# A smaller share of a convolution's lane for VectorE, closed by a product that GpSimd's additions wait for

## The chip, the cores and the metric

The kernel runs on one core of one Trainium2 chip. The metric is device time in microseconds of one execution. The engines are named as the profile names them: PE (TensorE matmul, with PEld for its weight loads), DVE (VectorE), ACT (ScalarE), POOL (GpSimd) and SP (SyncE, which here only issues transfers).

## The reference

Two operations follow each other. A depthwise causal convolution over the sequence, with 7 taps for each of 8 heads (the taps are a softmax of the given weights, 24 channels to a head):

```python
w = softmax(weight)                                  # (8 heads, 7 taps)
x_pad = concat([zeros((B, 6, D)), x], axis=1)        # B=8, S=4096, D=192
out[b, s, h, g] = sum_k w[h, k] * x_pad[b, s + k, h, g]
```

Then a gated feed-forward layer on its 32768 rows of 192, with 1536 hidden columns:

```python
gate = maximum(x @ w_gate, 0)
val = x @ w_val
return (gate * val) @ w_out                          # float32, (32768, 192)
```

## The kernel before, in words

The sequence is cut into 16 units of 1024 positions (UNIT) of two batches at once: batch b lies on partitions 0 to 63, batch b + 4 on 64 to 127. The 192 channels are three planes of 64, so the convolved input of a unit is a tile xc of 128 x 3 x 1024 in f16, or 3072 columns when it is read flat (FLAT).

**A unit's work on PE** has two stages. `gate_val` makes, for each of two windows of 512 and each of 12 blocks f of hidden columns, the gate and the value products (line 468, six matmuls each) into two PSUM tiles. ACT takes the gate through Relu to gr (line 477), DVE multiplies gr with the value's PSUM tile into hT (line 478). Then `project_columns` runs three times (p = 0, 1, 2), 96 matmuls each (line 488), into one PSUM tile each. DVE turns each of these (line 502, `turn_out`) into the output tile, and SP stores it when the third is done. All PSUM tiles named ps come from one pool with four buffers that are taken in turn, so a tile waits until the fourth tile before it has been read.

**The convolution of units 2 to 15** is made two units ahead, beside the projections, in what the code calls a lane. POOL loads x (`lane_load`), copies it into another order (`lane_turn`, line 387), and SP issues eight DMA transposes that make x_r, with channels on partitions and positions along the free axis, plus a halo of 16. From x_r each tap is a shifted read times a scale that differs by partition. The 3072 columns are divided at LDVE:

- Columns 0 to LDVE are DVE's. ACT makes the first tap into acc in f32 (`lane_first`, line 434), DVE adds the six others with one instruction each and piece (`lane_rest`, line 445: in0 * scalar + in1, inputs x_r and acc). The last tap writes xc in f16. A piece ends at a plane's end, so LDVE = 1408 gives two pieces per tap, 1024 and 384 columns: 12 instructions, handed out one at a time by a generator.
- Columns LDVE to FLAT are ACT's and POOL's. ACT multiplies each tap into a tile of its own, prod0 to prod6 in f32 (`product`, line 414, pieces of 640 and 1024), and POOL adds prod1 to prod6 onto prod0 one after the other (`add`, line 423), the last sum going to xc.

**The order** is written out by hand (`manual_schedule`): every engine works off its instructions in the order in which the code emits them. In the loop over units a lane stands around the projections of unit u for unit u + 2: `lane_first` on ACT, and then after each `project_columns` the products of the taps in TAPS[p], STEPS[p] of the lane's instructions on DVE, and the transpose. So DVE has 3 steps, a transpose, 4 steps, a transpose, 5 steps, a transpose, and then the 24 multiplications of line 478 of the next unit. ACT emits tap 0 last. POOL's first addition of a lane (prod0 + prod1) is emitted at the start of the next unit, ahead of the halo copy, the two copies to x_p, the two loads of x_e, four more additions and the one into xc. Each prod tile has one buffer.

Units 0 and 1 get their convolution on PE from band matrices (`conv_dense`, `conv`), and the last unit has another projection (`project`, line 524). Lanes run in the units 0 to 13; unit 0's addition is emitted in unit 1, and so on. Unit 0's projections have convolution work of unit 1 between them, on PE and on ACT.

Of the kernel before, what the change touches and what calls it, by code (L numbers as in the profile page):

```python
# [10 lines left out]
ACTF = mybir.ActivationFunctionType  # L11
ALU = mybir.AluOpType
# [3 lines left out]
def kernel(  # L16
# [12 lines left out]
    nc = tc.nc  # L29
# [10 lines left out]
    WIN = 512  # L40
    NWIN = S // WIN
    SUB = 112
    STEPS = [3, 4, 5]
    TAPS = [(6, 5, 4), (3, 2), (1, 0)]
    GSUB = 5

# [2 lines left out]
    NUNIT = NB * S // UNIT  # L49
    HALO = 16  # L50
    FLAT = NCH * UNIT
    LDVE = 1408
    TILES = UNIT // 128
    GROUPS = [(0, [WIN * w + SUB * j for j in range(GSUB)]) for w in range(2)]
    second = [min(t, 2 * UNIT - SUB) for t in range(UNIT, 2 * UNIT, SUB)]
# [55 lines left out]
    for half, eng in ((0, nc.sync), (1, nc.scalar)):  # L111
        eng.dma_start(
            out=wr[64 * half : 64 * half + 64],
            in_=bass.AP(
                tensor=weight.tensor,
                offset=weight.offset + 2 * half * HQ * KW,
                ap=[[HQ * KW, 2], [0, 32], [1, HQ * KW]],
            ),
# [8 lines left out]
    for n in range(16):  # L127
        nc.tensor.matmul(  # L128
            out=ps[:, n % 2, :], lhsT=zeros[:, 0:128], rhs=zeros[:], start=True, stop=True
# [9 lines left out]
    for q in range(4):  # L139
        nc.gpsimd.affine_select(  # L140
            out=eye[32 * q : 32 * q + 32],
            in_=ones[32 * q : 32 * q + 32],
# [55 lines left out]
    tap = const.tile([128, NCH, KW], FP)  # L198

    def load_taps():  # L200
# [23 lines left out]
        out=prod[:],  # L224
        in0=bass.AP(tensor=e0.tensor, offset=e0.offset, ap=[e0.ap[0], [0, HQ], [1, BW], [1, KW]]),
# [115 lines left out]
    xes, xrs, accs, prods = {}, {}, {}, {}  # L341
# [53 lines left out]
    def pieces(lo, hi):  # L395


        while lo < hi:
            c, t = lo // UNIT, lo % UNIT
            n = min(UNIT - t, hi - lo)  # L400
            yield lo, n, c, t
            lo += n

    def shifted(u, c, k, t, n):
        o = HALO - KW + 1 + k + t
        return xrs[u][:, c, o : o + n]

    def flat(u):
        return xc[u][:].rearrange("p c t -> p (c t)")

    def product(u, k):
        prods[u, k] = apool.tile([128, FLAT - LDVE], FP, name=f"prod{k}")
        for at, n, c, t in pieces(LDVE, FLAT):
            nc.scalar.activation(  # L414
                out=prods[u, k][:, at - LDVE : at - LDVE + n],
                in_=shifted(u, c, k, t, n),
                func=ACTF.Copy,
                scale=tap[:, c, k : k + 1],
            )

    def add(u, k):
        p0 = prods[u, 0]
        nc.gpsimd.tensor_tensor(  # L423
            out=p0[:] if k < KW - 1 else flat(u)[:, LDVE:FLAT],
            in0=p0[:],
# [4 lines left out]
    def lane_first(u):  # L430
        accs[u] = apool.tile([128, LDVE], FP, name="acc")
        xc[u] = xcpool.tile([128, NCH, UNIT], F16, name="xc")
        for at, n, c, t in pieces(0, LDVE):
            nc.scalar.activation(  # L434
                out=accs[u][:, at : at + n],
                in_=shifted(u, c, 0, t, n),
                func=ACTF.Copy,
                scale=tap[:, c, 0:1],
            )

    def lane_rest(u):
        acc = accs.pop(u)
        for k in range(1, KW):
            for at, n, c, t in pieces(0, LDVE):
                nc.vector.scalar_tensor_tensor(  # L445
                    out=(flat(u) if k == KW - 1 else acc)[:, at : at + n],
                    in0=shifted(u, c, k, t, n),
                    scalar=tap[:, c, k : k + 1],
                    in1=acc[:, at : at + n],
                    op0=ALU.mult,  # L450
                    op1=ALU.add,
                )
                yield

    def gate_val(u, w):
        h = hpool.tile([128, NFF, 2, WIN], F16, name="hT")
        xcb = xc[u]
        for f in range(NFF):
            if u == 0 and w == 0 and f == 7:
                conv_dense(1)  # L460
            pss = [psum.tile([128, 2, 512], FP, name="ps") for _ in range(2)]
            order = [(i, c) for i in range(2) for c in range(NCH)]
            if u == 0 and w == 0 and f == 0:
                order.sort(key=lambda ic: ic[1])
            for i, c in order:
                W = (Wg, Wv)[i]
                for st in range(2):
                    nc.tensor.matmul(  # L468
                        out=pss[i][:, st, :],
                        lhsT=W[64 * st : 64 * st + 64, c, 128 * f : 128 * (f + 1)],  # L470
                        rhs=xcb[64 * st : 64 * st + 64, c, WIN * w : WIN * (w + 1)],
                        start=(c == 0),
                        stop=(c == NCH - 1),
                        tile_position=(64 * st, 0),
                    )
            gr = gpool.tile([128, 2, WIN], F16, name="gr")
            nc.scalar.activation(out=gr[:], in_=pss[0][:], func=ACTF.Relu)  # L477
            nc.vector.tensor_tensor(out=h[:, f], in0=gr[:], in1=pss[1][:], op=ALU.mult)  # L478
        return h
# [67 lines left out]
    for u in range(NUNIT):  # L547
# [25 lines left out]
        if u + 2 < NUNIT:  # L573
            lane_first(u + 2)
            lane = lane_rest(u + 2)
# [5 lines left out]
        for p in range(3):  # L581
            ps = project_columns(hs, p)
            if lane:
                for k in TAPS[p]:
                    product(u + 2, k)
                for _ in range(STEPS[p]):
                    next(lane)
            turn_out(ps, o, p)
            if u == 0 and p == 0:
                conv(3)  # L590
# [31 lines left out]
```

## Time and profile before

| | before |
|---|---|
| time, median of 3 runs | 827.27 us (823.82 to 830.51) |
| profiled execution: its time / its span | 829.14 / 827.4 us |
| PE busy | 784.5 us, 95% |
| PEld busy | 401.2 us, 48% |
| DVE busy | 720.7 us, 87% |
| ACT busy | 599.2 us, 72% |
| POOL busy | 414.8 us, 50% |
| granted PE clock, mean | 0.973 |
| HBM read / written | 29.50 / 25.17 MB |

The span runs from the first to the last instruction of the profiled execution; the time holds some 1.7 us around it. Busy times are sums over an engine's own instructions and overlap between engines. In the rows a duration is in nanoseconds in the table of groups (busy us, mean ns of one, then the idle time ahead of them) and in microseconds in the order of time (start, length, engine, line, operation, output<-inputs with shapes, count, and in brackets the idle time ahead of it with what ended it). In a line of the waits stand who waited for whom, the total, how many times, and the longest. A row in the order of time that covers several instructions gives their whole stretch.

### The profile page before, as it was taken

The numbers are of one execution on the slowest core, as the hardware profiler recorded it, in microseconds if no ns is written. First come the engines' busy times: TensorE is split into PE (matmuls) and PEld (weight loads), VectorE is DVE, ScalarE is ACT, GpSimd is POOL, SyncE is SP. The second block draws the span as 40 slices with busy tenths as digits, with TensorE's granted clock in tenths as the row PEclk, the third lists the DMA queues.
The fourth block names the chain that finished last, engine by engine and source line by source line (L and its number), as shares of the span: only waits on it lengthen the run. The fifth ranks groups of instructions, "written<-read, shape, count | busy, mean of one in ns | idle before, by whom it ended". The sixth has DMA issues, their size and how long they took to land.

```text
span 827.4 us, 21544 instructions
## 1 busy us (share of the span) xinstructions
PE 784.5 (95%) x9392; PEld 401.2 (48%) x9392; DVE 720.7 (87%) x627; ACT 599.2 (72%) x635; POOL 414.8 (50%) x194
## 2 busy tenths in 40 slices
PE   8999989999899998989989899898998989989998
PEld 4554445445454454545545455454554545545447
DVE  7889989989899898998989989899898989988591
ACT  4798867868678685776858779586795867956372
POOL 9507666291762917529085390843908448091000
PEclk9999999999999999999999999999999999999999
DMA  9927538090370904609045090550906414030202
GB/s 107 137 52 126 78 62 93 2 143 12 67 88 2 144 11 75 80 2 153 2 85 71 6 150 2 95 60 14 140 3 105 50 23 93 3 77 2 66 13 77
DMA packets 123106, 53.20 MB, mean 64 GB/s; under 512 B 88692, under 2 KB 123012, under 8 KB 123012
## 3 DMA queue, kind: packets, MB, share of 16 engines
q1 hardware_dynamic: 84690, 36.99, 26.4%
q0 software_dynamic: 38112, 14.75, 17.1%
q8 instruction: 73, 1.20, 0.6%
q14 instruction: 21, 0.17, 0.1%
q10 hardware_dynamic: 210, 0.10, 0.0%
HBM read 29.50 MB, written 25.17 MB: 66 GB/s over the span
## 4 chain that ended last, share of the span: by engine, by line
PE 82%; DVE 13%; issue 3%; DMA 1%; ACT 0%; DVEq 0%
PE ps L468 59%; PE ps L488 20%; DVE xc L445 5%; DVE out_s L502 4%; DVE acc L445 3%; PE ps L524 2%; DMA wr<-in_weight_dram 1%; DVE hT L478 0%; ACT gr L477 0%; PE ps L304 0%; DVE band L242 0%; DVE prod L223 0%; DVE blk L231 0%; DVE xc L289 0%; DVE Wg L167 0%
## 5 line engine op out<-in xcount | busy, mean ns | idle before, releaser
L477 ACT ACTIVATE gr<-ps 128x1024 f16<-128x1024 f32 x384 | 392.8, 1023 | 203.8 <-PE ps L468 203.7
L478 DVE TENSOR_TENSOR hT<-gr,ps 128x1024 f16<-128x1024 f16 x384 | 468.1, 1220 | 53.3 <-ACT gr L477 19.0
L423 POOL TENSOR_TENSOR prod<-prod,prod 128x1664 f32<-128x1664 f32 x70 | 267.6, 3823 | 320.6 <-ACT prod L414 317.1
L468 PE MATMUL ps<-xc,Wv 64*128 64x512 f16 x2304 | 329.4, 388 | 36.1 <-DVE out_s L502 34.9
L468 PE MATMUL ps<-xc,Wg 64*128 64x512 f16 x2304 | 325.8, 385 | 0.4 <-DVE hT L478 0.2
L488 PE MATMUL ps<-hT,Wo 128*32 128x512 f16 x4320 | 236.0, 379 | 0.0
L468 PEld LDWEIGHTS <-Wv 64*128 64x128 f16 x2304 | 138.8, 96 | 160.3 <-issue 54.0
L468 PEld LDWEIGHTS <-Wg 64*128 64x128 f16 x2304 | 126.5, 96 | 133.0 <-issue 17.4
L414 ACT ACTIVATE prod<-x_r,tap 128x640 f32<-128x640 f16 x196 | 173.9, 977 | 0.0
L488 PEld LDWEIGHTS <-Wo 128*32 128x32 f16 x4320 | 114.1, 97 | 120.3 <-issue 6.3
L445 DVE SCALAR_TENSOR_TENSOR acc<-x_r,tap,acc 128x1024 f32<-128x1024 f16 (+1 forms) x140 | 123.3, 939 | 2.3 <-ACT acc L434 2.1
L502 DVE STREAM_TRANSPOSE out_s<-ps 128x1024 f32<-128x1024 f32 x45 | 56.1, 1246 | 29.0 <-PE ps L488 29.0
L445 DVE SCALAR_TENSOR_TENSOR xc<-x_r,tap,acc 128x1024 f16<-128x1024 f16 (+1 forms) x28 | 70.1, 2546 | 0.0
L423 POOL TENSOR_TENSOR xc<-prod,prod 128x1664 f16<-128x1664 f32 x14 | 51.9, 3708 | 1.1
L387 POOL COPY x_p<-x_e 128x1536 f16<-128x1536 f16 x28 | 41.0, 1490 | 2.1 <-DMA x_e<-in_x_dram 2.1
L350 POOL DMA_DIRECT2D x_e<-in_x_dram x28 | 25.0, 898 | 3.8 <-POOL x_p L387 3.6
L434 ACT ACTIVATE acc<-x_r,tap 128x1024 f32<-128x1024 f16 (+1 forms) x28 | 23.0, 872 | 0.2 <-issue 0.2
L524 PE MATMUL ps<-Wo,hT 128*128 128x192 f16 x192 | 16.0, 246 | 0.0
L524 PEld LDWEIGHTS <-hT 128*128 128x128 f16 x192 | 15.8, 98 | 0.4 <-issue 0.4
L535 ACT COPY out_s<-ps 128x768 f32<-128x768 f32 (+2 forms) x5 | 3.2, 639 | 12.7 <-PE ps L524 12.7
L535 DVE COPY out_s<-ps 128x192 f32<-128x192 f32 x1 | 0.4, 357 | 13.3 <-PE ps L524 13.3
L128 PE MATMUL ps<-zeros 128*128 128x512 f16 x16 | 6.1, 568 | 1.5 <-DVE zeros L125 1.5
(44 smaller groups left out, 62.6 us busy)
## 6 DMA issues: line engine op xcount, KB each, us to landing
out_dram<-out_s SPq DMA_DIRECT2D x63, 384.0 KB
x_e<-in_x_dram POOLq DMA_DIRECT2D x28, 384.0 KB, 10.8
x_r<-x_p SPq DMA_TRANSPOSE x112
out_s<-in_x_dram POOLq DMA_DIRECT2D x4, 240.0 KB, 7.1
out_s<-in_x_dram POOLq DMA_DIRECT2D x4, 192.0 KB, 4.4
Wo<-in_moe_w_out_dram POOLq DMA_DIRECT2D x1, 576.0 KB, 9.1
Wg<-in_moe_w_gate_dram POOLq DMA_DIRECT2D x3, 144.0 KB, 5.8
Wv<-in_moe_w_val_dram POOLq DMA_DIRECT2D x3, 144.0 KB, 5.1
```

The source lines that it names most:

```text
L350: nc.gpsimd.dma_start(out=xe[:, :, st, :, :].rearrange("p j c r -> p j (c r)"), in_=bass.AP(tensor=x.tensor, offset=x.offset + row * D, ap ...
L387: nc.gpsimd.tensor_copy(out=xp[:, :, :, st, :], in_=xe[:, :, st, :, :])
L414: nc.scalar.activation(out=prods[u, k][:, at - LDVE : at - LDVE + n], in_=shifted(u, c, k, t, n), func=ACTF.Copy, scale=tap[:, c, k : k + 1],)
L423: nc.gpsimd.tensor_tensor(out=p0[:] if k < KW - 1 else flat(u)[:, LDVE:FLAT], in0=p0[:], in1=prods.pop((u, k))[:], op=ALU.add,)
L434: nc.scalar.activation(out=accs[u][:, at : at + n], in_=shifted(u, c, 0, t, n), func=ACTF.Copy, scale=tap[:, c, 0:1],)
L445: nc.vector.scalar_tensor_tensor(out=(flat(u) if k == KW - 1 else acc)[:, at : at + n], in0=shifted(u, c, k, t, n), scalar=tap[:, c, k : k ...
L468: nc.tensor.matmul(out=pss[i][:, st, :], lhsT=W[64 * st : 64 * st + 64, c, 128 * f : 128 * (f + 1)], rhs=xcb[64 * st : 64 * st + 64, c, WI ...
L477: nc.scalar.activation(out=gr[:], in_=pss[0][:], func=ACTF.Relu)
L478: nc.vector.tensor_tensor(out=h[:, f], in0=gr[:], in1=pss[1][:], op=ALU.mult)
L488: nc.tensor.matmul(out=ps[32 * s : 32 * s + 32, b, :], lhsT=Wo[:, f, 64 * p + 32 * b : 64 * p + 32 * b + 32], rhs=hs[s // 2][:, f, s % 2, ...
L502: nc.vector.transpose(out=o[:, :, 64 * p : 64 * p + 64].rearrange("p t (b c) -> p b t c", b=2), in_=ps[:].rearrange("p b (t c) -> p b t c" ...
L524: nc.tensor.matmul(out=ps[:, i // 2, D * (i % 2) : D * (i % 2) + D], lhsT=h[:, f, st, 128 * q : 128 * (q + 1)], rhs=Wo[:, f, :], start=(f ...
```

## The change

LDVE goes from 1408 to 1280, so DVE's second piece of each tap has 256 columns in place of 384, ACT's first piece 768 in place of 640, and each of POOL's additions 1792 columns in place of 1664. For tap 0, ACT makes only the piece of 1024; the piece of 768 of prod0 is made by DVE, in a new last instruction of the lane. The lane thus has 13 instructions on DVE, handed out 4, 5 and 4. POOL's first addition of a lane reads all of prod0.

```diff
-    STEPS = [3, 4, 5]
+    STEPS = [4, 5, 4]
...
-    LDVE = 1408
+    LDVE = 1280
...
         for at, n, c, t in pieces(LDVE, FLAT):
-            nc.scalar.activation(
-                out=prods[u, k][:, at - LDVE : at - LDVE + n],
-                in_=shifted(u, c, k, t, n),
-                func=ACTF.Copy,
-                scale=tap[:, c, k : k + 1],
-            )
+            if k or t == 0:
+                nc.scalar.activation(
+                    out=prods[u, k][:, at - LDVE : at - LDVE + n],
+                    in_=shifted(u, c, k, t, n),
+                    func=ACTF.Copy,
+                    scale=tap[:, c, k : k + 1],
+                )
...
                 yield
+        at, n, c, t = next(pieces(LDVE, FLAT))
+        nc.vector.tensor_scalar(
+            out=prods[u, 0][:, 0:n],
+            in0=shifted(u, c, 0, t, n),
+            scalar1=tap[:, c, 0:1],
+            scalar2=None,
+            op0=ALU.mult,
+        )
+        yield
```

## The prediction

> **What bounds the kernel now.** I read the chain that ended last first, then the waits, then the groups with shapes kept apart, then one unit in order of time. The chain by engine, two groups and one wait:
>
> ```profile
> PE 82%; DVE 13%; issue 3%; DMA 1%; ACT 0%; DVEq 0%
> ```
>
> ```profile
> L445 DVE SCALAR_TENSOR_TENSOR xc<-x_r,tap,acc 128x384 f16<-128x384 f16 x14 | 53.4, 3812 | 0.0
> L445 DVE SCALAR_TENSOR_TENSOR acc<-x_r,tap,acc 128x384 f32<-128x384 f16 x70 | 41.9, 598 | 0.0
> ```
>
> ```profile
> PE ps L468 <- DVE out_s L502: 34.9, 13, 2.7
> ```
>
> TensorE (PE) is the chain, except for one visit to VectorE (DVE) per unit. There it waits for the transposes of line 502, 13 times, 2.7 us each. And the same DVE step on 128x384 takes 0.598 us when it writes acc, 3.812 us when it writes xc. One unit in order of time, DVE, then GpSimd (POOL), then PE:
>
> ```profile
> 261.53 1.81 DVE L445 SCALAR_TENSOR_TENSOR acc<-x_r,tap,acc 128x1024 f32<-128x1024 f16 x2
> 263.26 5.25 DVE L445 SCALAR_TENSOR_TENSOR xc<-x_r,tap,acc 128x1024 f16<-128x1024 f16 x2
> 268.43 1.24 DVE L502 STREAM_TRANSPOSE out_s<-ps 128x1024 f32<-128x1024 f32 x1
> ```
>
> ```profile
> 263.75 4.34 POOL L423 TENSOR_TENSOR prod<-prod,prod 128x1664 f32<-128x1664 f32 x1 [22.66 <-ACT prod L414]
> 268.04 0.55 POOL L377 COPY x_r<-x_r 128x48 f16<-128x48 f16 x1
> ```
>
> ```profile
> 264.93 0.82 PE L468 MATMUL ps<-xc,Wg 64*128 64x512 f16 x6
> 265.58 0.81 PE L468 MATMUL ps<-xc,Wv 64*128 64x512 f16 x6
> 266.23 0.81 PE L468 MATMUL ps<-xc,Wg 64*128 64x512 f16 x6
> 269.72 1.47 PE L468 MATMUL ps<-xc,Wv 64*128 64x512 f16 x6 [2.68 <-DVE out_s L502]
> 270.95 1.51 PE L468 MATMUL ps<-xc,Wg 64*128 64x512 f16 x6
> 272.23 1.14 PE L468 MATMUL ps<-xc,Wv 64*128 64x512 f16 x6
> 273.19 0.82 PE L468 MATMUL ps<-xc,Wg 64*128 64x512 f16 x6
> ```
>
> What to see: POOL's first addition starts at 263.75, inside DVE's last step but one. DVE's last step, 0.6 us of work, then stands until the addition ends at 268.09. The addition itself took 4.34 us where others take 3.71: it stood until DVE's running step was over. So a DVE step with two inputs in SBUF (x_r and acc) and such an addition exclude each other. The third transpose is behind the blocked step, and PE's fourth group needs the PSUM buffer that this transpose frees (four buffers: three projections, then two for each f; the second f's Wv takes the third projection's). In the first unit that has a lane, ScalarE (ACT) is late, the addition starts at 65.03, after DVE's lane, the 384-step has the group's least (0.61 us), and PE doesn't wait. DVE's rows there:
>
> ```profile
> 62.49 1.80 DVE L445 SCALAR_TENSOR_TENSOR xc<-x_r,tap,acc 128x1024 f16<-128x1024 f16 x2
> 64.27 1.25 DVE L502 STREAM_TRANSPOSE out_s<-ps 128x1024 f32<-128x1024 f32 x1
> ```
>
> **What a unit loses.** By the chain in order of time PE's projections start at 95.41 (unit 1) and 761.39 (unit 14): 13 units in 665.98 us, 51.23 each. Unit 14, without lane or wait, runs from 761.39 to 808.23: 46.84 us. The difference is 4.39 us. It adds up in the PE rows: from 266.23 to 269.72 are 3.49 us for a group that has 0.65, 2.84 lost; from 269.72 to 273.19 are 3.47 for three groups, 1.95 at full speed, 1.52 lost. The second loss is the granted clock: by the stretches it is 1.00 up to 266.9, 0.50 from 269.7 to 272.2, and 1.00 again from 273.2. So the wait costs its own length and a slow restart behind it.
>
> [...]
>
> **The change part by part.** All times are put on the unit that begins at 250.92 on DVE.
>
> *The lane's steps.* Six steps go from 384 to 256 elements. The rows of 1024 and 384 give (1279 - 598) / 640 = 1.064 ns an element, so 462 ns for 256: 6 x 136 = 0.82 us less. Back-to-back steps start some 0.085 us before the recorded end of the one before (261.04 to 263.26 is 2.22 us for 2.475 of durations), so I count 1.20, 0.38 and, for a 384-step, 0.52.
>
> *The added product* (128x768, f16 to f32, one input in SBUF and a scale) has no row of its form. Below: the 64x768 copy of line 167 at 11.93 took 0.42. Above: the two-input step by its line, 0.598 + 384 x 1.064 = 1.01, plus 0.15, as line 189's tensor_scalar on 2 elements took 0.32 where its neighbours took 0.17: 1.16. I take 1.01 (0.92 spaced), the nearest operation. DVE's work is then unchanged: 0.82 off, 0.92 on.
>
> *The order 4, 5, 4.* Four steps: 250.92 + 2 x (1.20 + 0.38) = 254.08. The first transpose waits for PE until 254.69, as before. Next step 255.86; five steps, 3 x 1.20 + 2 x 0.38 = 4.36: 260.22, so the second transpose is 0.35 later than now (259.87). It costs nothing: its buffer is wanted at 266.23. Then 261.39 + 0.38 + 1.20 + 0.38 + 0.92 = 264.27 is the end of the lane. PE ends the third projection at 264.93; with the 0.18 that lay between PE's end (249.27 + 15.72 / 3 = 254.51) and the first transpose, the third starts near 265.1 and ends near 266.35. PE wants that buffer at 266.9. So DVE has 0.8 us of room before the transpose and 0.55 behind it; the product's upper bound takes 0.15. If this cover were gone, each further us would be a wait of PE, with its slow restart.
>
> *What holds the addition.* It reads all of prod0, whose first 768 columns DVE now writes with its last instruction. So it can't start before 264.3, when no two-input step of DVE is left. That takes away the block: 3.2 us of DVE, and with it PE's wait. ACT's product ends about as now (263.6) and stops being what POOL waits for.
>
> *POOL.* Queued behind the held addition: the halo copy, two copies to x_p, the two loads of x_e, four additions and the one into xc. Additions grow from 1664 to 1792: between 0 and 7.7% (3.71 to 3.99 us), at most 6 x 0.28 = 1.7 us a unit. The chain starts 0.6 later, saves the 0.63 of standing, and ends at most 1.9 us later, at 294.2 instead of 292.35. The next lane starts on DVE at 250.92 + 46.84 = 297.8. So 3.5 us remain before it could meet the next lane, and ACT's next product of tap 6, which needs its buffer, comes later still. SP issues its four stores (4.54 us) when the third transpose ends, so by 270.9 in place of 274.2; its transposes of x_r (15.28 us) also wait for the copies to x_p, which end near 272 (now 271.4). They end near 287.3 (now 289.6), 9 us before ACT begins its next lane. Unit 1 is tightest: its last addition ends 0.7 us before the next lane now, and may reach it by 0.2; that is inside DVE's room.
>
> *ACT.* Same elements (6 x 128 more, 640 and 128 fewer), one instruction of some 0.28 us fewer. It isn't on the chain: nothing.
>
> **Sum.** 13 x 4.39 = 57.1 us. The profiled execution has 829.14 us (span 827.4): 772.0. The median shown is 827.27, which would give 770.2.
>
> **Rivals.** *1. The transpose takes the blocked step's place.* It would now start at 265.1 under an addition that runs from 264.4 to 268.4. If it were blocked like the step, it would end near 269.7, as now (269.67): 829, no change, up to 832 if each unit loses 0.2 more. For it: before shows no transpose that starts under an addition. Against: in unit 0 a transpose (64.27, 1.25 us) overlapped an addition that began at 65.03 and took 3.71 us, no longer than alone, and line 478's products, with one input in SBUF and one in PSUM, keep 1.22 us under all the other additions. [...]
>
> *2. Only the wait goes.* If the slow groups behind it had another cause, 13 x 1.71 us would stay and 13 x 2.68 = 34.8 go: 794. The same place covers a transpose that is still late by part of the 3.3 us. Against: units 0 and 14, without the wait, have no slow groups. [...]
>
> *3. The clock falls because PE never rests.* This is the one that ends slower. PE's 608.9 us of these 13 units would be stretched by 1/g; from g = 0.914 down there is no gain (608.9 / 665.98), and at 0.89 it is 684 us, 847 in all. Against: from 47.4 to 112 and from 274 to 317 PE worked without a pause at 1.00.
>
> *4. The change doesn't do what it says*: were the addition released by ACT's part alone, it would meet the two last steps as now: 829. In the built program the addition waits for both engines, so I count this within rival 1.
>
> **Chances.** Forecast 0.86, rival 1 (with 4) 0.05, rival 2 0.05, rival 3 0.04. A run of this kernel tells about 1% from no change. Faster by over 1%: 0.91; within 1%: 0.05; slower: 0.04. The range is the forecast's: below, 770.2 less the 3.4 us by which the lowest run lay under the median, 766; above, 772 and 0.75 us a unit for a late third transpose: 782. That holds about 0.83.
>
> **What would show it.** No wait of PE for line 502 and clock 1.00 throughout; DVE's last xc step near 0.46 us; POOL's first addition released by DVE's product, at about 4.0 us; PE's projections 46.8 to 46.9 us apart; POOL's last addition over before the next lane. I am wrong if the third transpose shows 3 us and more, if additions overlap steps of the next lane, or if the clock column has stretches under 1.00.

## The result and the profile after

The changed kernel takes 772.33 us (median of 4 runs, 771.74 to 772.66) where the kernel before takes 827.91 beside it (4 runs): the ratio is 0.933, with a 95% interval of 0.929 to 0.937. The profiled execution took 772.0 us, its span is 770.3.

The chain by engine, and the chain's pieces in order of time (start, length, engine, tile, line, count) over three units:

```profile
PE 97%; DVE 1%; DMA 1%; ACT 0%; issue 0%; DVEq 0%
```

```profile
188.98 15.65 PE ps L498 x288
204.63 31.19 PE ps L478 x288
235.82 15.65 PE ps L498 x288
251.47 31.19 PE ps L478 x288
282.66 15.65 PE ps L498 x288
```

DVE has gone from 13% of the chain to 1%. The projections (now line 498) follow each other at 46.84 us, the figure that only unit 14 had before; of PE waiting for the transposes nothing is left. One unit in order of time, DVE and POOL:

```profile
249.80 0.62 DVE L456 TENSOR_SCALAR prod<-x_r,tap 128x768 f32<-128x768 f16 x1
251.53 1.25 DVE L512 STREAM_TRANSPOSE out_s<-ps 128x1024 f32<-128x1024 f32 x1 [1.11 <-PE ps L498]
253.32 1.22 DVE L488 TENSOR_TENSOR hT<-gr,ps 128x1024 f16<-128x1024 f16 x1 [0.55 <-ACT gr L487]
```

```profile
250.56 3.99 POOL L424 TENSOR_TENSOR prod<-prod,prod 128x1792 f32<-128x1792 f32 x1 [17.58 <-DVE prod L456]
254.49 0.22 POOL L377 COPY x_r<-x_r 128x48 f16<-128x48 f16 x1
```

The addition starts when DVE's product is done, and the third transpose waits for PE, no longer for DVE. This transpose runs wholly under the addition and takes its usual 1.25 us. (In 12 of the 14 lanes DVE's product releases the addition; in the first two ACT's product comes last, and there too DVE's lane is over by then.) Two groups of the changed kernel with shapes kept apart:

```profile
L446 DVE SCALAR_TENSOR_TENSOR xc<-x_r,tap,acc 128x256 f16<-128x256 f16 x14 | 6.7, 482 | 0.0
L456 DVE TENSOR_SCALAR prod<-x_r,tap 128x768 f32<-128x768 f16 x14 | 8.7, 618 | 0.0
```

The last step of a lane is now 0.48 us in every unit. Before, it was 3.81 us as a mean of 14 lanes; the first of them, which was not blocked, took 0.61 us, so the 13 others took 4.06 each ((53.4 - 0.61) / 13).

### The profile page after: what moved, and what is told of

It reads as the page before. It is cut to its first block, busy times and chain, and to the rows that moved or that the text cites. A ratio compares the mean times of both kernels' runs of the same rounds, so it can differ in the third digit from the quotient of the medians.

```text
span 770.3 us, 21536 instructions
## 1 busy us (share of the span) xinstructions
PE 762.6 (99%) x9392; PEld 381.7 (50%) x9392; DVE 674.6 (88%) x641; ACT 596.8 (77%) x621; POOL 425.6 (55%) x194
## 4 chain that ended last, share of the span: by engine, by line
PE 97%; DVE 1%; DMA 1%; ACT 0%; issue 0%; DVEq 0%
PE ps L478 65%; PE ps L498 30%; PE ps L534 2%; DMA wr<-in_weight_dram 1%; PE ps L304 0%; DVE band L242 0%; DVE Wg L167 0%; DVE Wv L167 0%; DVE hT L488 0%; ACT gr L487 0%; DVE prod L223 0%; DVE blk L231 0%; DVE xc L289 0%; ACT out_s L545 0%; DVE sm L189 0%
## 5 line engine op out<-in xcount | busy, mean ns | idle before, releaser
L424 POOL TENSOR_TENSOR prod<-prod,prod 128x1792 f32<-128x1792 f32 x70 | 278.4, 3977 | 258.2 <-DVE prod L456 212.9
L478 PE MATMUL ps<-xc,Wg 64*128 64x512 f16 x2304 | 314.2, 376 | 0.6 <-DVE hT L488 0.2
L478 PE MATMUL ps<-xc,Wv 64*128 64x512 f16 x2304 | 314.1, 376 | 0.6 <-DVE Wv L167 0.3
L478 PEld LDWEIGHTS <-Wv 64*128 64x128 f16 x2304 | 131.8, 94 | 118.5 <-issue 1.3
L478 PEld LDWEIGHTS <-Wg 64*128 64x128 f16 x2304 | 114.4, 94 | 137.1 <-issue 7.0
L415 ACT ACTIVATE prod<-x_r,tap 128x1024 f32<-128x1024 f16 (+1 forms) x182 | 172.8, 1040 | 0.0
L446 DVE SCALAR_TENSOR_TENSOR acc<-x_r,tap,acc 128x1024 f32<-128x1024 f16 (+1 forms) x140 | 114.0, 873 | 2.8 <-ACT acc L435 2.8
L424 POOL TENSOR_TENSOR xc<-prod,prod 128x1792 f16<-128x1792 f32 x14 | 55.7, 3982 | 1.1
L446 DVE SCALAR_TENSOR_TENSOR xc<-x_r,tap,acc 128x1024 f16<-128x1024 f16 (+1 forms) x28 | 23.5, 882 | 0.0
L456 DVE TENSOR_SCALAR prod<-x_r,tap 128x768 f32<-128x768 f16 x14 | 8.7, 618 | 0.0
```

What stands on the lines that cost most here:

```text
L415: nc.scalar.activation(out=prods[u, k][:, at - LDVE : at - LDVE + n], in_=shifted(u, c, k, t, n), func=ACTF.Copy, scale=tap[:, c, k : k + 1],)
L424: nc.gpsimd.tensor_tensor(out=p0[:] if k < KW - 1 else flat(u)[:, LDVE:FLAT], in0=p0[:], in1=prods.pop((u, k))[:], op=ALU.add,)
L446: nc.vector.scalar_tensor_tensor(out=(flat(u) if k == KW - 1 else acc)[:, at : at + n], in0=shifted(u, c, k, t, n), scalar=tap[:, c, k : k ...
L478: nc.tensor.matmul(out=pss[i][:, st, :], lhsT=W[64 * st : 64 * st + 64, c, 128 * f : 128 * (f + 1)], rhs=xcb[64 * st : 64 * st + 64, c, WI ...
```

## The experiments

The theory under test (A): a POOL addition that has started shuts out DVE's next two-input step for its whole length; the blocked step makes the third transpose late, and PE waits. Nothing else of the change matters. The rival (B): the hold of the addition by DVE's product is what frees DVE, and the split and the order alone would leave the block.

### The parts one by one

**The split and the order, without the hold.** Against the changed kernel:

```diff
-    STEPS = [4, 5, 4]
+    STEPS = [4, 5, 3]
...
-            if k or t == 0:
...
-        at, n, c, t = next(pieces(LDVE, FLAT))
-        nc.vector.tensor_scalar(...)
-        yield
```

> The change without its hold: LDVE 1280 and the order 4, 5, 3, but ACT makes all of prod0 and the added product is left out, so ACT alone releases POOL's first addition. Theory A (all that matters is that no two-input step of DVE comes after the start of the addition): by the rows of the changed kernel DVE's last step ends near 249.8, while ACT, with one product of 768 more (0.92 us), ends near 250.8 and the addition starts near 250.9, so they don't meet: 772 us. Theory B (the hold by DVE's product is what frees DVE): without it the addition meets the last step as before: 825 to 831 us.

Measured: 772.41 us, ratio 0.933 (0.930 to 0.936). The addition, released by ACT, starts at 251.44 in its profile; DVE's lane is over at 250.45.

**The order alone.** Against the kernel before:

```diff
-    STEPS = [3, 4, 5]
+    STEPS = [4, 5, 3]
```

> The order alone: LDVE stays 1408, no added product, steps 4, 5, 3. By the rows of before DVE's last step (384) would start near 263.4 and the addition at 263.75, 0.35 us later, so theory A expects the addition to stand for 0.25 us and DVE not at all: 772 us, by a narrow margin. Theory B: 825 to 831 us.

Measured: 772.00 us, ratio 0.932 (0.930 to 0.935). DVE's and POOL's rows in order of time:

```profile
248.61 1.81 DVE L445 SCALAR_TENSOR_TENSOR xc<-x_r,tap,acc 128x1024 f16<-128x1024 f16 x2
251.52 1.25 DVE L502 STREAM_TRANSPOSE out_s<-ps 128x1024 f32<-128x1024 f32 x1 [1.11 <-PE ps L488]
```

```profile
250.23 3.76 POOL L423 TENSOR_TENSOR prod<-prod,prod 128x1664 f32<-128x1664 f32 x1 [19.16 <-ACT prod L414]
```

The last step (384 columns, 0.61 us, ending at 250.42) had started some 0.4 us ahead of the addition. The addition stood for 0.05 us, DVE not at all.

**The split alone.** Against the kernel before:

```diff
-    LDVE = 1408
+    LDVE = 1280
```

> The split alone: LDVE 1280, steps 3, 4, 5 as before, ACT makes all of prod0. In the times of before DVE's last step (256) would start near 264.2, and ACT's last product end near 264.3 with the addition at 264.4. Theory A leaves it to these 0.2 us: 772 us if the step comes first, 829 to 833 us if the addition does, and nothing between unless units differ. Theory B: 825 to 831 us.

Measured: 773.31 us, ratio 0.934 (0.931 to 0.937). The step came first, narrowly. DVE's and POOL's rows:

```profile
250.92 1.68 DVE L445 SCALAR_TENSOR_TENSOR xc<-x_r,tap,acc 128x1024 f16<-128x1024 f16 x2
```

```profile
252.33 4.10 POOL L423 TENSOR_TENSOR prod<-prod,prod 128x1792 f32<-128x1792 f32 x1 [17.45 <-ACT prod L414]
```

The addition starts at 252.33, DVE's lane ends at 252.60, and the addition takes 4.10 us where the others of the run take 3.98. So it was the addition that stood, by 0.12 us, and almost alike (4.10 to 4.12 us) in every lane from the third on.

**The hold alone.** Against the kernel before, 16 columns of tap 0 are made once more by DVE at the lane's end:

```diff
-    STEPS = [3, 4, 5]
+    STEPS = [3, 4, 6]
...
                 yield
+        at, n, c, t = next(pieces(LDVE, FLAT))
+        nc.vector.tensor_scalar(
+            out=prods[u, 0][:, 0:16],
+            in0=shifted(u, c, 0, t, 16),
+            scalar1=tap[:, c, 0:1],
+            scalar2=None,
+            op0=ALU.mult,
+        )
+        yield
```

> The hold alone: LDVE 1408 and ACT's products as before; at the lane's end DVE makes 16 columns of tap 0 in prod0 once more, so that POOL's first addition has to wait for it; steps 3, 4, 6. Both theories expect the block to go. By the rows of before the lane then ends near 265.3, the third transpose at 266.6, and PE wants its buffer at 266.9: 772 us, up to 776 if the transpose is late by up to 0.3 us. A theory by which the smaller share or the order did it expects 829.

Measured: 771.87 us, ratio 0.932 (0.930 to 0.935). The added instruction takes 0.23 us; the third transpose starts at 251.79, without waiting for PE.

B falls. Each of the three parts alone brings the whole gain, because each alone moves DVE's last two-input step ahead of the addition: the split by 0.2 us, the order by 0.4, the hold by construction.

### Bringing the meeting back

**One more step on DVE, with the order alone.** Against the order alone; the step's result is read by nobody:

```diff
-    STEPS = [4, 5, 3]
+    STEPS = [4, 5, 4]
...
         for k in range(1, KW):
+            if k == KW - 1:
+                nc.vector.scalar_tensor_tensor(
+                    out=idle[:],
+                    in0=shifted(u, 0, 0, 0, UNIT),
+                    scalar=tap[:, 0, 0:1],
+                    in1=acc[:, 0:UNIT],
+                    op0=ALU.mult,
+                    op1=ALU.add,
+                )
+                yield
```

> The order alone (LDVE 1408, no product of DVE's own in prod0) with one more two-input step of 1024 on DVE, whose result nobody reads, between the second transpose and the last tap. The changed kernel took one more such step without loss. Here nothing holds POOL's first addition: it is released by ACT, in the times of the run with the order alone at 250.2, and DVE's last step now comes to 251.0, behind it. Theory A (an addition that has started shuts out DVE's next two-input step for its whole length): the last step shows about 3.8 us again, PE waits 2.7 us, and the time is back near 829. If the order itself had made the kernel immune: 772 to 773.

**The same step with the hold.** Against the kernel with the hold alone, the same added step and another order:

```diff
-    STEPS = [3, 4, 6]
+    STEPS = [4, 5, 5]
```

> The same step more, with the order 4, 5, 5 and the hold of 16 columns: POOL's first addition waits for DVE's last instruction. LDVE is 1408, so DVE's lane is 1.2 us longer than in the run with the order alone and 0.13 for the small product: it ends near 251.8, the third transpose near 253.0 to 253.1, and PE wants the buffer at 253.4. Theory A: no block, 772 us, up to 776. Without the hold's effect: 829.

Measured: 829.25 us without the hold, ratio to the kernel before 1.003 (1.000 to 1.006), and 771.62 with it, ratio 0.931 (0.929 to 0.934). The rows without the hold, POOL, a group of DVE, and a wait:

```profile
264.05 4.43 POOL L423 TENSOR_TENSOR prod<-prod,prod 128x1664 f32<-128x1664 f32 x1 [22.65 <-ACT prod L414]
```

```profile
L456 DVE SCALAR_TENSOR_TENSOR xc<-x_r,tap,acc 128x384 f16<-128x384 f16 x14 | 53.4, 3812 | 0.0
```

```profile
PE ps L479 <- DVE out_s L513: 35.8, 13, 2.8
```

The last step has the kernel before's mean of 3812 ns to the digit, and PE's 13 waits are back. With the hold the same group has 611 ns and PE waits for no transpose. A step that costs 1.2 us, and that fits into DVE's room, costs 57 us if it moves DVE's last step behind the start of the addition.

### How long the block lasts, and what it blocks

**The first addition in two halves.** Against the kernel before, in `add`, with p1 for the popped tile:

```diff
-        nc.gpsimd.tensor_tensor(
-            out=p0[:] if k < KW - 1 else flat(u)[:, LDVE:FLAT],
-            in0=p0[:],
-            in1=prods.pop((u, k))[:],
-            op=ALU.add,
-        )
+        n = FLAT - LDVE
+        cut = n // 2 if k == 1 else n
+        for lo in range(0, n, cut):
+            nc.gpsimd.tensor_tensor(
+                out=p0[:, lo : lo + cut] if k < KW - 1 else flat(u)[:, LDVE:FLAT],
+                in0=p0[:, lo : lo + cut],
+                in1=p1[:, lo : lo + cut],
+                op=ALU.add,
+            )
```

> The kernel before with POOL's first addition cut into two instructions of 832 columns. If an addition that is running excludes DVE's step for its whole length and no longer, the last step (384) waits for the first half only, which runs from about 264.4 to 266.3; it is over near 266.9, the third transpose near 268.1, and PE loses 1.2 us in place of 2.84, with or without the slow restart of 1.5: between 788 and 808 us, and the last step shows about 2.4 us in place of 3.81. If the two share time instead of excluding each other, the step keeps 3.8 us and the time stays near 829.

Measured: 787.19 us in one run. The last step takes 2.18 us, and the wait of PE is 0.93 us:

```profile
L449 DVE SCALAR_TENSOR_TENSOR xc<-x_r,tap,acc 128x384 f16<-128x384 f16 x14 | 30.6, 2182 | 0.0
```

```profile
258.28 0.82 PE L472 MATMUL ps<-xc,Wv 64*128 64x512 f16 x6 [0.93 <-DVE out_s L506]
```

So here the step waited for the one instruction that was running and slipped in ahead of the second half: in this unit the first half ends at 256.66 and the step at 257.07. The clock stayed at 1.00, so the loss is little more than the wait: a unit takes 1.1 us more (258.28 - 256.54 is 1.74 us for a group that has 0.65), 13 x 1.1 = 14.3, and 772 + 14.3 = 786, just under the lower end of what was expected.

**One-input steps at the lane's end.** Against the order alone, three products of 128x640 (f16 to f32, the added product's operation) into a tile that nobody reads:

```diff
-    STEPS = [4, 5, 3]
+    STEPS = [4, 5, 6]
...
                 yield
+        for _ in range(3):
+            nc.vector.tensor_scalar(
+                out=idle[:, 0:640],
+                in0=shifted(u, 1, 0, 384, 640),
+                scalar1=tap[:, 1, 0:1],
+                scalar2=None,
+                op0=ALU.mult,
+            )
+            yield
```

> The order alone with three steps of one input behind the lane (the added product's operation, 128x640, f16 to f32, into a tile that nobody reads), so that they meet POOL's first addition. By their own length (0.5 us each) they fit into DVE's room. If a step with one SBUF input is not shut out: 772 to 773. [...]

Measured: 876.26 us in one run, 103 above the 773 that go with a step that is not shut out. DVE's last two-input step and the first of the three, the three together, and POOL:

```profile
272.44 0.61 DVE L446 SCALAR_TENSOR_TENSOR xc<-x_r,tap,acc 128x384 f16<-128x384 f16 x1
272.96 4.00 DVE L456 TENSOR_SCALAR idle<-x_r,tap 128x640 f32<-128x640 f16 x1
```

```profile
272.96 7.50 DVE L456 TENSOR_SCALAR idle<-x_r,tap 128x640 f32<-128x640 f16 x3
280.39 1.23 DVE L512 STREAM_TRANSPOSE out_s<-ps 128x1024 f32<-128x1024 f32 x1
```

```profile
272.86 3.76 POOL L423 TENSOR_TENSOR prod<-prod,prod 128x1664 f32<-128x1664 f32 x1 [26.48 <-ACT prod L414]
276.56 0.49 POOL L377 COPY x_r<-x_r 128x48 f16<-128x48 f16 x1
276.99 3.13 POOL L387 COPY x_p<-x_e 128x1536 f16<-128x1536 f16 x2
```

The first step is shut out by the addition (4.00 us in place of 0.55, the shortest of the 42), and the two behind it took 3.5 us beside POOL's copies, where 0.55 each would be 1.1. PE then waits 5.5 us in this unit, and behind the wait three groups take 1.46 to 1.51 us and one 1.08 where others take 0.82; the mean granted clock of the run is 0.945. So the operation of the added product was shut out as well, with one input. In the changed kernel, where it takes 0.62 us, it is safe because the addition waits for it, not because it has one input.

### What a wait of PE costs

The changed kernel with more two-input steps of 1024 ahead of the product (into acc, which is dead by then), n = 1 to 4, and n more in the third number of STEPS:

```diff
+        for _ in range(n):
+            nc.vector.scalar_tensor_tensor(
+                out=acc[:, 0:UNIT],
+                in0=shifted(u, 0, 0, 0, UNIT),
+                scalar=tap[:, 0, 0:1],
+                in1=acc[:, 0:UNIT],
+                op0=ALU.mult,
+                op1=ALU.add,
+            )
+            yield
```

One more:

> The changed kernel with one more two-input step of 1024 on DVE ahead of the lane's product (into acc, which nobody reads any more; it adds nothing to the result). By the rows of the changed kernel DVE is idle for 1.1 us before the third transpose, and PE wants its buffer 0.6 us after the transpose ends. A step costs 1.2: no wait, 772 us.

Two more:

> As the run before it with two more steps: the third transpose ends near 254.0, PE loses about 0.7 us in each of 14 units, 10 us: 782. If even this wait brings the slow restart that followed the 2.7 us waits (1.5 us each), 803.

Three more:

> The changed kernel with three more steps of 1024: between the waits of 0.6 us (two steps, clock stays at 1.00) and of 2.6 us (four steps, clock 0.50 for 3.4 us behind each). PE's wait is 1.2 to 1.9 us. If it doesn't bring down the clock: 14 times the wait and 0.16, 791 to 801. If it does: 3.4 us at half clock cost up to 1.7 us more per unit, 815 to 833.

Four more:

> As before with four more steps: PE loses about 3.1 us in each of 14 units, 43 us: 816 without a slow restart, 837 with 1.5 us of it per unit. [...]

Measured, one run each:

| steps more | time, us | waits of PE for a transpose | mean granted clock |
|---|---|---|---|
| 0 | 772.33 | none | 1.000 |
| 1 | 772.57 | none of 0.9 us or more | 0.998 |
| 2 | 784.88 | 12 of 0.6 us, one of 0.3, one of 2.68 | 1.000 |
| 3 | 801.50 | 14 of 1.9 us | 1.000 |
| 4 | 831.96 | 13 of 2.6 us, one of 2.3 | 0.973 |

The first step is free within the spread of the runs (772.57, where the changed kernel has 771.74 to 772.66), as DVE's room foretold. The second and third cost their waits and 0.2 us for each; both came out a little above what was expected, with two steps by 2.9 us, most of it the 2.68 us wait of unit 1. The fourth adds 30 us for 0.7 us more of wait in each unit: now the clock falls, to 0.50 behind the wait in the unit shown here (from 273.0 to 276.2), and to 0.973 as the mean of the run. Its time lies between the two that were expected, as its wait is 2.6 us and not 3.1. Three rows of PE with four steps more:

```profile
273.14 1.46 PE L488 MATMUL ps<-xc,Wg 64*128 64x512 f16 x6 [2.61 <-DVE out_s L522]
274.38 1.51 PE L488 MATMUL ps<-xc,Wv 64*128 64x512 f16 x6
275.66 1.19 PE L488 MATMUL ps<-xc,Wg 64*128 64x512 f16 x6
```

In this build it is PE's fifth group after the projections that waits, in the others the fourth, so its wait is 0.65 us shorter than the steps alone would make it.

## Why the prediction was right

772.0 was forecast, 772.33 measured. The saving was forecast as 57.1 us; it is 57.1 between the two profiled executions and 55.6 between the medians. By its own steps:

- **What a unit loses** (4.39 us, of which 2.84 wait and 1.52 slow groups): all of it went. The projections of the units 1 to 14 are 46.84 us apart, as predicted, and the clock is 1.00 throughout.
- **The added product** was taken at 1.01 us, between 0.42 and 1.16. It takes 0.62. With 0.23 for 16 columns in the run with the hold alone, that is (618 - 230) / 752 = 0.52 ns an element, half of the two-input step's 1.064. The size was off by 0.39 us, at a place where it is hidden: DVE was idle for 1.11 us ahead of the third transpose, against 0.8 predicted.
- **The order.** The third transpose ends 0.6 us before PE wants its buffer (251.53 + 1.25 = 252.78, and 253.36); 0.55 was predicted.
- **POOL.** The additions take 3.98 us with 1792 columns, where 1664 took 3.71: the upper end of 3.71 to 3.99. The last addition of a unit ends 42.4 us after DVE's lane begins (237.41 to 279.82); at most 43.3 was predicted. 0.33 us of this is the halo copy, which takes 0.22 now and took 0.55 before, when DVE's blocked step ran beside its start.
- **Unit 1** had a wait that the prediction didn't name: ACT waits 0.79 us for the transposes of x_r before its lane, and DVE starts 0.72 late. It was covered, as the third transpose there still waits 0.88 us for PE. The delay also hid that the forecast for this unit was too low: the last addition of the lane before ends at 97.73, and DVE's lane begins at 97.69. A lane begun 0.72 earlier would have met that addition for some 0.7 us, not for the 0.2 that was feared.

**One step was wrong, and it cost nothing: "What holds the addition", which says that the hold takes away the block.** The runs with the split, the order, or both show that the block goes without it. The prediction's own numbers held this: its schedule has the lane's last two-input step over at 264.27 - 0.92 = 263.35, and ACT's last product at 263.6. Yet it did not work out from them what would happen without the hold, and rival 4 put that case at 829; the run with the split and the order, where ACT alone releases the addition, has 772.41. What the hold does is shown by the pair with one step more, 771.62 against 829.25: it turns a lead that depends on durations (0.2 us with the split alone, 0.4 with the order alone) into an order that the program fixes.

Of the rivals, the transpose in the blocked step's place (1) is refuted by the transpose that ran wholly under an addition in 1.25 us. The clock that falls without rest (3) did not come: 1.00 over the whole span. "Only the wait goes" (2) is refuted by the time, but the runs with more steps show that it had asked a fair question: the runs whose waits are 0.6 us (two steps more, one wait of 2.68 aside), 0.9 (the addition in halves) and 1.9 (three steps more) have a mean granted clock of 1.000, those with 2.6 to 2.8 (before, the order with one step more, four steps more) one of 0.973. The kernel before, with 2.68, is among the latter. Had its wait been 1.9 us, the same change would have been worth some 27 us and not 57. This is an estimate from the run with three steps more, where a unit costs (801.50 - 772.33) / 14 = 2.08 us: 13 x 2.08.

## What to carry to other kernels

Where an engine's step is several times as long as its twins and shows no idle time ahead of it (here 3.81 us against 0.60, with 0.0 idle), look at what runs beside it on the other engine: the block of this case stood inside the duration, not among the waits. Here it was decided by who started first: leads of 0.2 and 0.4 us kept the step free, and 1.2 us of work in the wrong place cost 57. If a lead is that small, make the order certain with a data dependency, as the product does here. And ask of each part of a change what the rest would do without it, from the same schedule.

## What the runs showed of the hardware that was not expected

**The block lasted for whole instructions, and met not only two-input steps.** Under a first addition of 1664 columns the last two-input step took 3.81 us as a mean, under one in halves of 832 columns 2.18, and 0.61 where nothing blocked it. The one-input product from f16 to f32 was shut out by an addition (4.00 us for 0.55) and slowed beside copies (3.5 us for two), while a transpose from PSUM (1.25 us) and a multiplication with one input in SBUF and one in PSUM (1.22) ran under additions at their usual length.

**The clock fell in stretches of 3.41 us, 51.20 us apart.** In the kernel before, the clock is 0.50 from 115.85 to 119.26, from 269.45 to 272.86 and from 730.24 to 733.65: 3.41 us each time, as the stretch in the middle shows (us, busy times, and then the clock):

```profile
269.45:272.86 3.41, 3.14 (x16) 1.37 (x17) 2.54 (x3) 0.36 (x1) 3.11 (x4) 0.50 0.56 125
```

The starts of these stretches are 153.60 and 460.79 us apart, 3 and 9 times 51.20; all 13 stretches of the kernel before are 3.41 us long and start 51.20 us apart. PE's restarts after the waits come to the same distance: they are 51.39, 51.29, 51.25 and 51.22 us apart in the first units, and 51.19 to 51.22 in the later ones. With four steps more, where PE's waits are 2.61 us and not 2.68, the projections in late units are 51.20 us apart too:

```profile
610.61 15.65 PE ps L508 x288
661.80 15.65 PE ps L508 x288
713.00 15.65 PE ps L508 x288
764.20 15.65 PE ps L508 x288
```

With the order and one step more, PE's waits are some 2.75 us, and the mean granted clock is 0.973 as in the kernel before and with four steps more. With the one-input steps, where PE waits 5.7 us as a mean of 13, it is 0.945, and the projections of late units are 54.6 us apart.

What sets these distances was not shown, nor whether a small saving could vanish in them: no run took a small step within one such kernel. The length of a wait alone did not decide whether the clock fell: with four steps more it fell behind a wait of 2.61 us, while one of 2.68 us, in the run with two steps more, left it at 1.00, as did one of 2.28 in the run with four.
